# An earlier gather for the first expert, and the first attention heads in another order

## The chip, the cores and the metric

The kernel runs on one core of a Trainium2 chip. Its time is the device time of one execution in microseconds (us). TensorE (PE, with its weight loads as PEld), VectorE (DVE), ScalarE (ACT) and GpSimd (POOL) each work through their own instructions in order; SyncE (SP) issues most of the DMAs, also in order.

## The reference

Three stages, each feeding the next, all in float32.

```
scores = q @ k.T / 8 + (cum[i] - cum[j]),  cum = cumsum(log(clip(f, 1e-4, 1)))   # 4 batches, 8 heads, 576 rows, 64 wide
attn   = softmax over j <= i;  x = attn @ v          -> (2304, 512)
x      = (sigmoid(x @ w_gate) * (x @ w_val)) @ w_out -> (2304, 512), 1536 wide inside
logits = x @ moe2_w_gate                             -> (2304, 8)
# all 18432 (token, expert) pairs in falling order of logit: a pair is taken
# if the token is still free and the expert has under 288 tokens
out[tokens of e] = relu(x[tokens of e] @ w1[e]) @ w2[e]      # 8 experts, 512 -> 1024 -> 512
```

## The kernel before

Products that need more than one pass of precision are made from a high part (`hi`, rounded to fp32r) and a rest (`lo`), as hi·hi + hi·lo + lo·hi.

**Attention** (`attention`) goes through 32 heads. For a head, `load` brings q and k of a pair of heads into `raw` (576 KB), `prep` (ACT, L128) rounds them into `P1`, `prep2` (POOL, L141 and L142) forms the rest in `P2`, and `copies` (SP, L136 and L137) sends `P1` to the other half of `P2`. `P1` has three more rows: two of the decay (`cum`, split in two) or of ones, and a third that holds the negated row maxima. `maxpass` multiplies q by k in blocks into three PSUM banks and takes row maxima on DVE (L169); `mrows` turns them on PE, ACT copies them (L176), and `mstore` (SP, L179) writes them into row 66 of `P1`. Only then can `scores` run for that head: PE multiplies, ACT takes exp (L199), POOL zeroes what lies above the diagonal (L203). `av` multiplies by v. In the steady part one pass of the loop issues scores of head h, then av of head h-1 with the maxima of head h+3 placed between its matmuls. The first heads are written out by hand ahead of the loop; the order of the whole attention is the order of the code, on each engine. `warm` issues matmuls into a bank that nobody reads. `fill` places the first steps of the next stage's weights between heads: `W.load` (SP, L386, 512 KB each), `W.bits` (three DVE steps, L394 to L400), `W.cut` (ACT L408, POOL L411).

**Feed-forward** (`Ffn`) keeps the weights in SBUF, and works in five groups of tokens. The last product of the last 6 token tiles is put off: `defer` is a generator of 252 matmul steps (L666), each tile 36 steps, the last tile (tokens 15 of 18) as two halves of 36. Its result is copied by ACT (L669) into `xd` and stored to `x2d` in DRAM (L513).

**Routing** (`Route`) finds the assignment by 7 rounds on DVE and PE; `filler` puts deferred matmuls between them. `permutation` writes `idx`, the token numbers of each expert. Beside the rounds, `EW.split` prepares the first four weight tiles of the first expert.

**Experts** (`experts`): three indirect DMAs on POOL (`gather`, L991) fetch the 288 tokens of an expert from `x2d` in pieces of 96, PE turns them (`turn`, L1001), ACT and DVE split them (L1004, L1005), then two layers follow (L1015, L1028). A `gather` waits for every earlier store into `x2d`. For the first expert it stands behind the last store; 27 matmuls (L1056) that nobody reads stand on PE meanwhile. Four more weight tiles are loaded by ACT's queue (L949) behind the turned tokens, and split by ACT, POOL and DVE (L971, L973) during the first layer.

Of the kernel before, what the change touches and what calls it, by code (L numbers as in the profile page):

```python
# [34 lines left out]
def make_consts(ev, pool, keep):  # L35

    nc = ev.nc

    jp = pool.tile([128, 128], I32, name="jp")
    nc.gpsimd.iota(jp, pattern=[[1, 128]], base=0, channel_multiplier=-1)  # L40
    ev.identb = pool.tile([128, 128], BF16, name="identb")
    nc.vector.tensor_scalar(ev.identb, jp, 0.0, None, op0=OP.is_equal)
    ev.mk = pool.tile([128, 512], BF16, name="mk")
    nc.vector.memset(ev.mk, 1.0)
# [16 lines left out]
WARM = (22, 4, 2, 2)  # L61
# [3 lines left out]
def attention(ev, qkT, vr, f, xs, rec, ckd, fill):  # L65
# [4 lines left out]
    with ExitStack() as ctx:  # L70
# [27 lines left out]
        zero = st.tile([NHEAD, 1], F32, name="zero")  # L98
        nc.gpsimd.memset(zero, 0.0)
        next(consts)  # L100
# [8 lines left out]
        ck = st.tile([NHEAD, 2, S], F32R, name="ck")  # L109
        nc.vector.tensor_scalar(ft, ft, 1e-4, 1.0, op0=OP.max, op1=OP.min)  # L110
        nc.scalar.activation(ft, ft, AF.Ln)
        next(consts)
# [4 lines left out]
        for t in P1[2:]:  # L117
            nc.vector.memset(t[64:67].bitcast(F32), 1.0)
# [32 lines left out]
        def maxpass(h):  # L151

            p1 = P1[h % 4]
            a = ps1.tile([128, 512], F32, name="p1b")
            c = ps1.tile([128, 512], F32, name="p1b")
            b = MT[h] = ps2.tile([128, 1024], F32, name="pb")
            q = lambda s, e: p1[0:66, Q0 + s:Q0 + e]
            k = lambda s, e: p1[0:66, K0 + s:K0 + e]
# [3 lines left out]
            mm(c[:, 448:512], q(-64, 64), k(0, 64), False, True)  # L162
            mm(b[:, 256:512], q(448, 576), k(0, 256), True, True)
            mm(b[:, 512:832], q(448, 576), k(256, 576), True, True)
            mx = MR[h] = wk.tile([128, 5], F32R, name="mx", bufs=3)
            for t, src in ((1, a[:, 0:192]), (2, a[:, 192:512]), (3, c[:, 0:448]), (0, c[:, 448:512]),
                           (4, b[:, 256:832])):
                n = src.shape[-1]
                nc.vector.tensor_tensor_reduce(out=junk[:, JT[t]:JT[t] + n], in0=src, in1=ev.mq[:, S - n:], op0=OP.add,  # L169
                                               op1=OP.min, scale=-1.0, scalar=3e38, accum_out=mx[:, t:t + 1])  # L170
# [76 lines left out]
        def warm(n):  # L247

            t = ps2.tile([128, 1024], F32, name="pv")
            for _ in range(n):  # L250
                mm(t[:, 0:512], ev.identb, ev.mk, True, True)
# [7 lines left out]
        idle = st.tile([NHEAD, 1], F32, name="warm")  # L259
# [12 lines left out]
        prep2(1)  # L272
        ones(2)
        ones(0)
        for h in (2, 3):
            prep(h)
# [15 lines left out]
        load_v(1)  # L292
        load(3)
        decays(3)
        for h in range(1, NHEAD):
            odd = h % 2
            scores(h, 3 if h == 2 else None)
            if h == 2:
                mstore(3)
                next(consts)  # L300

            def rows(r):
                if r < NHEAD:
                    mrows(r)
                    mstore(r)

            def early():
                rows(h + 2 if h > 1 else 2)
                if h + 4 < NHEAD:
                    prep(h + 4)  # L310

            def late():
                if h + 3 < NHEAD:
                    maxpass(h + 3)

            if h == 1:
                av(0, {2: early, 3: lambda: maxpass(3)})
            elif h == 2:
                av(1, {0: lambda: maxpass(4), 5: early})
                late()  # L320
            else:
                av(h - 1, {AT[0]: early, AT[1]: late})
            if h < NHEAD - 3:
                copies(h + 3)
            if h >= 3 and odd:
                store(h // 2 - 1)
            if not odd and h // 2 + 3 < NPAIR:
                load(h // 2 + 3)
                decays(h // 2 + 3)
            if odd and h // 2 + 2 < NPAIR:  # L330
                load_v(h // 2 + 2)
# [6 lines left out]
            if h in (1, 2):  # L338
                fill(h - 3)
            fill(h)  # L340
# [361 lines left out]
class Route:  # L702
# [195 lines left out]
    def permutation(self, a):  # L898
# [5 lines left out]
        st = wk.tile([128, 2, NT], F32, name="r_st", bufs=1)  # L904
        nc.vector.tensor_reduce(st[:, 0], sl.rearrange("p e t -> p t e"), op=OP.add, axis=AX.X)
# [18 lines left out]
        return idx  # L924


class Experts:
# [9 lines left out]
    def load(self, n, queue=None):  # L937
        queue = queue or self.ev.nc.sync
        e, i = divmod(n, 8)
        if e < E:  # L940
            if n < 4:
                r = self.raw[n] = self.first.tile([128, 1024], F32, name="fraw", bufs=2)
            else:
                r = self.raw[n] = self.pool.tile([128, 1024], F32, name="eraw", bufs=RAWS)
            if i < 4:
                queue.dma_start(r, self.w1[e, i * 128:(i + 1) * 128, :])
            else:
                i -= 4
                queue.dma_start(r.rearrange("p (k d) -> p k d", k=2),  # L949
                                          self.w2[e, i * 256:(i + 1) * 256, :].rearrange("(k p) d -> p k d", p=128))  # L950

    def split(self, n, part=None, after=None):

        if part is not None:
# [7 lines left out]
            if part:  # L962
                del self.raw[n]
                if n < 2:
                    self.load(n + 2)
# [12 lines left out]
WAIT = 27  # L978


def experts(ev, W, x2d, idx, out, wk, psum):
    nc = ev.nc
    XG, XE, Y, T = {}, {}, {}, {}
# [11 lines left out]
    def turn(e, k, p=None, tiles=(0, 1, 2)):  # L995
        if k == 0 and tiles[0] == 0:
            XE[e] = [wk.tile([128, 4, CH], F32R, name=n) for n in ("xeh", "xel")]
        xh, xl = XE[e]
        p = p or psum("t")
        for i in tiles:  # L1000
            nc.tensor.transpose(p[:, i * TT:(i + 1) * TT], XG[e][i][:, k * 128:(k + 1) * 128], ev.ident[:TT, :TT])  # L1001
        if tiles[-1] < 2:
            return
# [53 lines left out]
    p = [psum(n) for n in "ttty"]  # L1057
    for i in range(3):
        for k in range(4):
            turn(0, k, p[k], (i,))  # L1060
# [39 lines left out]
def network(tc, qk, vv, f, ww, bcT, w1, w2, cb, cf, out):  # L1100
# [3 lines left out]
    with ExitStack() as ctx:  # L1104
# [25 lines left out]
        def fill(h):  # L1130
# [8 lines left out]
            count = lambda h: 3 + (h - 3) * (EARLY - 1) * 3 // 27  # L1139
            jobs = lambda h: range(count(h), count(h + 1))  # L1140
            for lag, do in enumerate((W.bits, lambda n, s: s == 2 and W.cut(n, (0,)),
                                      lambda n, s: s == 2 and W.cut(n, (1,)))):
                if 3 <= h - lag < 30:
# [33 lines left out]
        rest = F.defer(xd)  # L1177

        def filler(n):
            for _ in range(n):  # L1180
                if next(rest, 0) == 0:
                    break

        R = Route(ev, rp, rw, F.bank, cb, cf, scratch, filler)
        EW.load(0)
        EW.load(1)
# [15 lines left out]
        experts(ev, EW, x2d, ev.idx, out, xw, lambda n: pools[n].tile([128, 512], F32, name="e" + n))  # L1202
# [30 lines left out]
```

## Time and profile before

| | us |
|---|---|
| three runs | 935.55, 935.75, 939.06; median 935.75 |
| profiled execution, its own time | 935.39 |
| span of that execution | 933.4 |
| PE busy in the span | 911.9 (98%) |

A row of a group or of the timeline is one line of the kernel on one engine, what it writes and reads, how often, and how long it was busy. A bracket at its end says how long the engine stood idle before it and what released it. SPq, ACTq and POOLq rows are the issuing of DMAs. The granted clock of PE is given as a share of 2.4 GHz: 1.00 is 2.4 GHz, 0.50 is 1.2 GHz.

### The profile page before, as it was taken

How to read it: one execution, taken by the hardware profiler on the slowest of the kernel's cores; microseconds unless marked ns; L12 is line 12 of the kernel's file. 1: busy time of each engine (PE TensorE's matmuls, PEld its weight loads, DVE VectorE, ACT ScalarE, POOL GpSimd, SP SyncE). 2: the span in 40 equal slices, each digit the busy share in tenths (PEclk: the TensorE clock that was granted, in tenths of full speed). 3: DMA queues.
4: the chain of work that ended last, by engine and by line, in shares of the span. 5: the costliest groups of instructions: out<-in, count | busy, mean ns of one | idle time of the engine just before them, and what ended most of it. 6: DMA issues, size and time to landing. Idle time of an engine off the chain costs nothing. (4 is left out here: it accounts for less than half of the span.)

```text
span 933.4 us, 14077 instructions
## 1 busy us (share of the span) xinstructions
PE 911.9 (98%) x5187; PEld 767.1 (82%) x5188; DVE 550.2 (59%) x1188; ACT 330.7 (35%) x570; POOL 456.3 (49%) x388
## 2 busy tenths in 40 slices
PE   7999999999999999999999999999989999999996
PEld 4677777778788888888888888887779999999995
DVE  6467879736887287997979642535504433434431
ACT  4366666652323112121121221221116544444530
POOL 5578888853566113221222221322138787777641
PEclk7699999999999999999999999999999999999998
DMA  5688898764553202101021210011128765656610
GB/s 124 143 217 218 210 226 230 201 170 149 161 162 107 74 0 71 38 19 56 17 76 41 65 46 1 1 55 46 47 82 268 223 188 176 201 179 199 204 41 26
DMA packets 48873, 111.04 MB, mean 119 GB/s; under 512 B 11331, under 2 KB 11747, under 8 KB 48803
## 3 DMA queue, kind: packets, MB, share of 16 engines
q1 hardware_dynamic: 44642, 98.59, 37.7%
q0 software_dynamic: 3072, 9.44, 3.0%
q10 hardware_dynamic: 1088, 2.10, 0.7%
q8 instruction: 41, 0.67, 0.3%
q14 instruction: 30, 0.24, 0.1%
HBM read 86.12 MB, written 14.45 MB: 108 GB/s over the span
## 5 line engine op out<-in xcount | busy, mean ns | idle before, releaser
L497 POOL TENSOR_TENSOR gl<-sg,gh 128x512 fp32r<-128x512 f32 x36 | 50.0, 1388 | 200.9 <-ACT gh L496 200.9
L973 POOL TENSOR_TENSOR elo<-eraw,ehi 128x1024 fp32r<-128x1024 f32 x45 | 108.1, 2411 | 42.3 <-ACT ehi L971 41.9
L145 PE MATMUL pv<-e,vf 128*65 128x256 f32 (+1 forms) x434 | 108.6, 376 | 0.0
L490 PE MATMUL gv<-xah,w_hi 128*128 128x512 f32 (+1 forms) x288 | 103.3, 359 | 0.0
L490 PE MATMUL gv<-xal,w_hi 128*128 128x512 f32 (+1 forms) x288 | 103.0, 358 | 0.0
L490 PE MATMUL gv<-xah,w_lo 128*128 128x512 f32 (+1 forms) x288 | 102.9, 357 | 0.0
L530 DVE CUSTOM_DVE_ANT_0 mb<-mb,bc 128x512 f32<-128x512 f32 x96 | 82.2, 856 | 3.3
L530 DVE CUSTOM_DVE_ANT_0 mb<-mr,bc 128x512 f32<-128x512 f32 x96 | 82.4, 858 | 2.8
L1015 PE MATMUL eh<-xeh,ehi 128*128 128x288 f32 x256 | 78.8, 308 | 0.1
L496 ACT ACTIVATE gh<-sg 128x512 fp32r<-128x512 f32 x36 | 22.8, 633 | 156.5 <-PE o L509 84.4
L1028 PE MATMUL ey<-hh,ehi 128*128 128x288 f32 x256 | 78.1, 305 | 0.0
L1015 PE MATMUL eh<-xel,ehi 128*128 128x288 f32 x256 | 77.0, 301 | 0.0
L1015 PE MATMUL eh<-xeh,elo 128*128 128x288 f32 x256 | 76.8, 300 | 0.0
L1028 PE MATMUL ey<-hl,ehi 128*128 128x288 f32 x256 | 76.5, 299 | 0.0
L490 PE MATMUL gv<-xbh,w_hi 128*128 128x512 f32 x192 | 76.2, 397 | 0.0
L490 PE MATMUL gv<-xbl,w_hi 128*128 128x512 f32 x192 | 76.1, 396 | 0.0
L490 PE MATMUL gv<-xbh,w_lo 128*128 128x512 f32 x192 | 76.1, 396 | 0.0
L1028 PE MATMUL ey<-hh,elo 128*128 128x288 f32 x256 | 75.8, 296 | 0.0
L169 DVE CUSTOM_DVE_ANT_0 mj<-p1b,mq 128x192 bf16<-128x192 f32 (+3 forms) x128 | 46.8, 420 | 47.1 <-PE p1b L145 47.1
L145 PE MATMUL p1b<-P 66*128 66x192 f32 (+7 forms) x256 | 69.4, 340 | 2.8 <-DMA P<-ck 1.5
L145 PEld LDWEIGHTS pv<-e,vf 128*65 128x65 f32 x434 | 51.4, 142 | 24.9 <-issue 16.7
L1018 DVE SCALAR_TENSOR_TENSOR hl<-eh,hh 128x288 fp32r<-128x288 f32 x64 | 29.1, 456 | 61.6 <-ACT hh L1017 61.6
(204 smaller groups left out, 2285.2 us busy)
## 6 DMA issues: line engine op xcount, KB each, us to landing
eraw<-w SPq DMA_DIRECT2D x56, 512.0 KB
mr<-ww SPq DMA_DIRECT2D x26, 512.0 KB
raw<-qk SPq DMA_DIRECT2D x16, 576.0 KB
p<-P SPq DMA_DIRECT2D x64, 144.0 KB
vf<-vv SPq DMA_DIRECT2D x16, 330.0 KB
bc<-ww SPq DMA_DIRECT2D x10, 512.0 KB
xs<-xo SPq DMA_DIRECT2D x16, 292.5 KB
xr<-rec SPq DMA_DIRECT2D x32, 128.0 KB
```

Source lines behind the costliest of these rows:

```text
L145: nc.tensor.matmul(out, lhsT, rhs, start=start, stop=stop, skip_group_check=True)
L169: nc.vector.tensor_tensor_reduce(out=junk[:, JT[t]:JT[t] + n], in0=src, in1=ev.mq[:, S - n:], op0=OP.add, op1=OP.min, scale=-1.0, scalar=3 ...
L490: nc.tensor.matmul(p[i][:, :m], w_[:, ws], x_[:, k], start=n == 0, stop=n == 11)
L496: nc.scalar.activation(hi, s, AF.Copy)
L497: nc.gpsimd.tensor_tensor(lo, s, hi, op=OP.subtract)
L530: nc.vector.tensor_tensor_reduce(out=junk, in0=a, in1=self.bc[j], op0=OP.mult, op1=OP.add, scale=1.0, scalar=0.0, accum_out=res)
L973: eng.tensor_tensor(lo, r, hi, op=OP.subtract)
L1015: nc.tensor.matmul(p[:, :CH], w_[:, ws], x_[:, k], start=n == 0, stop=n == 11)
L1018: nc.vector.scalar_tensor_tensor(h[1][:, f], p[:, :CH], 0.0, h[0][:, f], op0=OP.max, op1=OP.subtract)
L1028: nc.tensor.matmul(p[:, :CH], w_[:, ws], h_[:, f], start=n == 0, stop=n == 23)
```

## The change

Two places change; lines of the changed code have other numbers, since it is 43 lines longer.

At the head of attention: the ones in `P1` are set by POOL and no longer by DVE; the constant tile `mk` goes (the warm matmuls read the identity instead); ACT runs one small Ln ahead of the first real one; 19, 4, 6, 2 warm matmuls stand where 22, 4, 2, 2 stood; the maxima of head 1 are issued in two parts with `mrows` of head 0 between them; `prep` and `copies` of heads 2 to 4, the memsets `ones` and the loads of pair 3 and of v change places; the first weight loads and their steps move from ahead of heads 1, 1 and 2 to the ends of heads 2, 4 and 5, and the later weight steps begin at head 5 and not 3 (42 steps over 25 heads, not 27).

At the first expert: zeros are stored into the rows of token tile 15 in `x2d` early, the gather of the first expert is issued when the two halves of tile 15 are still to be multiplied, and its missing rows are added by a matmul of `xd` with a 0/1 matrix `hot`. This turn uses ordinary float32 matmuls with the identity, not transposes. The 27 matmuls go. `fraw`, which holds raw weights of the first expert, has one buffer and not two.

```
-WARM = (22, 4, 2, 2)
+FIRST = {2: -3, 4: -2, 5: -1}
+WARM = (19, 4, 6, 2)
...
         for t in P1:
+            nc.gpsimd.memset(t[64:67].bitcast(F32), 1.0)
             nc.gpsimd.memset(t[0:64, 0:64].bitcast(F32), 0.0)
-        for t in P1[:2]:
-            nc.vector.memset(t[64:67].bitcast(F32), 1.0)
...
+        ones(1)
         copies(0)
+        prep2(0)
         maxpass(0)
         warm(WARM[1])
-        prep2(0)
-        ones(1)
         decays(1)
         copies(1)
+        prep2(1)
+        first = maxparts(1)
+        next(first)
         mrows(0)
         mstore(0)
-        maxpass(1)
+        next(first)
+        prep(2)
+        prep2(2)
         warm(WARM[2])
-        prep2(1)
-        ones(2)
-        ones(0)
-        for h in (2, 3):
-            prep(h)
         mrows(1)
         mstore(1)
         scores(0)
-        maxpass(2)
-        warm(WARM[3])
+        prep(3)
         load_v(0)
-        load(2)
         copies(2)
         decays(2)
-        for h in (2, 3):
-            prep2(h)
+        load(2)
         copies(3)
-        prep(4)
-        prep2(4)
-        fill(-3)
-        load_v(1)
-        load(3)
-        decays(3)
+        warm(WARM[3])
+        maxpass(2)
+        prep2(3)
+        ones(2)
...
+            if h in FIRST:
+                fill(FIRST[h])
...
+        self.xg = [t[:TT] for t in (slots[:, :DM], slots[:, DM:], big)]
...
+    def gather(self, route):
+        for i in range(3):
+            nc.gpsimd.indirect_dma_start(out=self.xg[i], out_offset=None, in_=self.x2d, ...)
+        nc.gpsimd.iota(places, pattern=[[1, CH]], base=0, channel_multiplier=0)
+        nc.vector.tensor_scalar(self.hot[:, :CH], places, route.slot[:, LAST:LAST + 1], None, op0=OP.is_equal)
+    def turn(self, x, bank):
+        for k in range(4):
+            ks = slice(k * 128, (k + 1) * 128)
+            p = bank()
+            for i in range(3):
+                nc.tensor.matmul(p[:, i * TT:(i + 1) * TT], self.xg[i][:, ks], self.ev.ident[:TT, :TT], start=i == 0, ...)
+            nc.tensor.matmul(p[:, :CH], x[:, ks], self.hot[:, :CH], start=False, stop=True, skip_group_check=True)
+            nc.scalar.activation(self.x[0][:, k], p[:, :CH], AF.Copy)
+            nc.vector.tensor_tensor(self.x[1][:, k], p[:, :CH], self.x[0][:, k], op=OP.subtract)
...
-    gather(0)
-    p = psum("h")
-    for _ in range(WAIT):
-        nc.tensor.matmul(p, W.hi[0][:, :128], W.hi[0][:, :512], start=True, stop=True)
...
+        nc.vector.memset(xd, 0.0)
+        F.store(LAST, xd)
...
+        filler(left - 2 * 3 * NF)
+        X0 = First(ev, ep, scratch, x2d)
+        X0.gather(R)
         for part in range(2):
             EW.split(3, part, ev.idx[:1, :1])
-        filler(1000)
+        filler(left)
+        next(rest, 0)
+        X0.turn(xd, F.bank)
```

What stood on PE at the maxima of heads 0 and 1, before (`P_0`, `P_1` are the operands of heads 0 and 1, `mx` the maxima, `pv<-mk,identb` a warm matmul):

```order
L145 MATMUL pv<-mk,identb 128x512
L145 MATMUL pb<-identr,mx 5x128
L145 MATMUL p1b<-P_1_117 128x192
L145 MATMUL p1b<-P_1_117 128x320
L145 MATMUL p1b<-P_1_117 128x448
L145 MATMUL p1b<-P_1_117 128x64
L145 MATMUL pb<-P_1_117 128x256
L145 MATMUL pb<-P_1_117 128x320
```

And in the changed kernel:

```order
L143 MATMUL pv<-identb 128x512
L143 MATMUL p1b<-P_1_117 128x192
L143 MATMUL p1b<-P_1_117 128x320
L143 MATMUL p1b<-P_1_117 128x448
L143 MATMUL p1b<-P_1_117 128x64
L143 MATMUL pb<-identr,mx 5x128
L143 MATMUL pb<-P_1_117 128x256
L143 MATMUL pb<-P_1_117 128x320
```

The turning of head 0's maxima moved behind four of head 1's matmuls.

What SP issued before head 2's maxima (`P_2_118<-mr`), before; `mr<-ww` is a weight load, `raw` a load of q and k, `vf` one of v, `p_...<-P` a copy:

```order
L136 DMA p_230<-P_3_119 64x576
L137 DMA p_230<-P_3_119 64x576
L386 DMA mr_290<-ww 128x512
L386 DMA mr_292<-ww 128x512
L93 DMA vf<-vv 128x660
L84 DMA raw_103<-qk 64x2x1152
L89 DMA raw_103<-ckd 2x2x576
L179 DMA P_2_118<-mr 1x5x128
```

And in the changed kernel:

```order
L83 DMA raw_105<-qk 64x2x1152
L134 DMA p_255<-P_3_119 64x576
L135 DMA p_255<-P_3_119 64x576
L188 DMA P_2_118<-mr 1x5x128
L134 DMA p_315<-P_0_116 64x576
L135 DMA p_315<-P_0_116 64x576
L83 DMA raw_103<-qk 64x2x1152
L88 DMA raw_103<-ckd 2x2x576
L92 DMA vf<-vv 128x660
```

Two weight loads, one of v and one of q and k moved from ahead of head 2's maxima to behind them.

What stands on PE in the changed kernel between the last turned k-block and the first expert's first layer (`mr` are the gathered tokens and `xd`, `mb` is `hot`):

```order
L1020 MATMUL gv<-ident,mr_5456 128x96 x2
L1020 MATMUL gv<-ident,mr_5455 128x96
L1022 MATMUL gv<-mb_5458,mr_5455 128x288
L1059 MATMUL eh<-xe0h,ehi_5597 128x288
L1059 MATMUL eh<-xe0l,ehi_5597 128x288
L1059 MATMUL eh<-xe0h,elo_5598 128x288
```

Each of four such k-blocks has three matmuls with the identity and one with `hot`, and the deferred matmuls stand right ahead of the first.

## Rows read from the trace of the kernel before

**Rows 1.** The page's first part: busy us, share of the span, instructions.

```profile
PE 911.9 (98%) x5187; PEld 767.1 (82%) x5188; DVE 550.2 (59%) x1188; ACT 330.7 (35%) x570; POOL 456.3 (49%) x388
```

**Rows 2.** Waits of PE over the span: us in total, times, longest us.

```profile
PE et L1001 <- DMA xg<-x2d,idx: 3.0, 3, 1.7
...
PE p1b L145 <- DVE mx L169: 1.1, 1, 1.1
```

**Rows 3.** Stretches of 1 us: PE, PEld, DVE, ACT, POOL busy; then clock, DMA, GB/s.

```profile
13.00:14.00 1.00, 0.65 (x3) 0.65 (x4) 0.29 (x2) 0.34 (x2) 0.94 (x2) 0.50 0.40 97
...
33.00:34.00 1.00, 0.40 (x1) 0.00 (x0) 1.00 (x1) 0.56 (x1) 0.93 (x2) 0.77 1.01 203
...
37.00:38.00 1.00, 1.00 (x6) 0.97 (x6) 0.00 (x0) 0.70 (x2) 0.00 (x0) 0.50 0.16 51
...
43.00:44.00 1.00, 1.00 (x5) 0.48 (x3) 0.00 (x0) 0.00 (x0) 0.00 (x0) 0.65 0.00 0
```

**Rows 4.** Timeline of PE, first heads: start us, us busy, line, operation.

```profile
10.50 0.74 PE L145 MATMUL p1b<-P 66*128 66x192 f32 x4 [1.54 <-DMA P<-ck]
...
13.35 0.27 PE L145 MATMUL pb<-identr,mx 128*5 128x128 f32 x1 [0.89 <-DVE mx L169]
...
16.57 0.52 PE L145 MATMUL py<-P 67*128 67x256 f32 x1
...
35.68 0.39 PE L145 MATMUL py<-P 67*128 67x256 f32 x1 [2.28 <-DMA P<-mr]
...
45.74 0.28 PE L145 MATMUL py<-P 67*128 67x256 f32 x1
...
47.50 1.13 PE L145 MATMUL pv<-e,vf 128*65 128x256 f32 x4
...
56.73 0.52 PE L145 MATMUL py<-P 67*128 67x256 f32 x1
```

**Rows 5.** Timelines of DVE, ACT and SP in the same stretch.

```profile
4.66 0.45 DVE L110 TENSOR_SCALAR ft<-ft 32x576 f32<-32x576 f32 x1
...
7.72 0.75 DVE L116 SCALAR_TENSOR_TENSOR ck<-cum,ck 32x576 fp32r<-32x576 f32 x1
...
6.96 2.22 ACT L128 ACTIVATE P<-raw 64x1152 fp32r<-64x1152 f32 x2 [1.13 <-DMA raw<-qk]
...
0.82 0.40 SPq L77 DMA_DIRECT2D ft<-f  x1
...
8.49 1.46 SPq L132 DMA_DIRECT2D P<-ck  x2
...
28.71 0.76 SPq L179 DMA_DIRECT2D P<-mr  x1
```

**Rows 6.** Timeline of PE at the first expert.

```profile
622.76 1.50 PE L653 MATMUL gv<-fold,mr 16*128 16x8 f32 x12
...
685.40 6.32 PE L1056 MATMUL eh<-ehi 128*128 128x512 f32 x27
...
695.86 0.74 PE L1001 MATMUL et<-ident,xg 96*128 96x96 f32 x3 [0.68 <-DMA xg<-x2d,idx]
...
696.78 0.61 PE L1015 MATMUL eh<-xeh,ehi 128*128 128x288 f32 x1
```

**Rows 7.** Timelines of ACT and POOL there.

```profile
677.02 0.60 ACT L669 ACTIVATE mr<-o 128x512 f32<-128x512 f32 x1 [6.42 <-PE o L666]
...
685.60 0.38 ACT L669 ACTIVATE mr<-o 128x256 f32<-128x256 f32 x1 [3.88 <-PE o L666]
...
690.04 1.13 POOL L991 DMA_INDIRECT xg<-x2d,idx  x1 [10.53 <-issue]
...
692.70 0.92 POOL L991 DMA_INDIRECT xg<-x2d,idx  x1 [0.31 <-issue]
```

**Rows 8.** Stretches of 2 us at the first expert, columns as in rows 3.

```profile
694.00:696.00 2.00, 0.69 (x5) 0.51 (x6) 0.00 (x0) 0.00 (x0) 1.46 (x2) 0.91 0.44 121
...
702.00:704.00 2.00, 2.00 (x15) 2.00 (x15) 0.46 (x1) 1.18 (x3) 1.60 (x1) 0.88 1.01 271
```

More of the change, by code (lines that the diff above doesn't have):

```diff
@@ L98, in attention @@
         zero = st.tile([NHEAD, 1], F32, name="zero")
+        idle = st.tile([NHEAD, 1], F32, name="warm")
         nc.gpsimd.memset(zero, 0.0)
+        nc.scalar.activation(idle, zero, AF.Ln, bias=1.0)
         next(consts)
@@ L162, in maxpass @@
             mm(c[:, 448:512], q(-64, 64), k(0, 64), False, True)
+            for t, src in ((1, a[:, 0:192]), (2, a[:, 192:512]), (3, c[:, 0:448]), (0, c[:, 448:512])):
+                top(t, src)
+            yield
+            b = MT[h] = ps2.tile([128, 1024], F32, name="pb")
             mm(b[:, 256:512], q(448, 576), k(0, 256), True, True)
             mm(b[:, 512:832], q(448, 576), k(256, 576), True, True)
[L165 to L170, printed above, removed]
+            top(4, b[:, 256:832])
+            yield
+        def maxpass(h):
+            for _ in maxparts(h):
+                pass
         def mrows(h):
@@ L297, in attention @@
             scores(h, 3 if h == 2 else None)
+            if h == 1:
+                ones(0)
             if h == 2:
@@ L308, in early @@
                 rows(h + 2 if h > 1 else 2)
-                if h + 4 < NHEAD:
+                if h == 1:
+                    prep(4)
+                    prep2(4)
+                elif h + 4 < NHEAD:
                     prep(h + 4)
@@ L317, in attention @@
                 av(0, {2: early, 3: lambda: maxpass(3)})
+                prep(5)
             elif h == 2:
@@ L326, in attention @@
                 store(h // 2 - 1)
+            if h == 1:
+                load(3)
+                decays(3)
             if not odd and h // 2 + 3 < NPAIR:
@@ L941, in load @@
             if n < 4:
-                r = self.raw[n] = self.first.tile([128, 1024], F32, name="fraw", bufs=2)
+                r = self.raw[n] = self.first.tile([128, 1024], F32, name="fraw", bufs=1)
             else:
@@ L963, in split @@
                 del self.raw[n]
-                if n < 2:
-                    self.load(n + 2)
+                if n < 3:
+                    self.load(n + 1)
         elif n < 8 * E:
@@ L977, with __init__, experts @@
 RAWS = 4
-WAIT = 27
-def experts(ev, W, x2d, idx, out, wk, psum):
+LAST = 15
+class First:
+    def __init__(self, ev, pool, scratch, x2d):
+        nc = self.nc = ev.nc
+        big, slots, self.places, self.hot = scratch
+        self.ev, self.x2d = ev, x2d
+        self.xg = [t[:TT] for t in (slots[:, :DM], slots[:, DM:], big)]
+        self.x = [pool.tile([128, 4, CH], F32R, name=n) for n in ("xe0h", "xe0l")]
+    def gather(self, route):
+        nc = self.nc
+        for i in range(3):
+            nc.gpsimd.indirect_dma_start(out=self.xg[i], out_offset=None, in_=self.x2d,
+                                         in_offset=bass.IndirectOffsetOnAxis(ap=self.ev.idx[:, i:i + 1], axis=0))
+        places = self.places[:, :CH].bitcast(I32)
+        nc.gpsimd.iota(places, pattern=[[1, CH]], base=0, channel_multiplier=0)
+        nc.vector.tensor_scalar(self.hot[:, :CH], places, route.slot[:, LAST:LAST + 1], None, op0=OP.is_equal)
+    def turn(self, x, bank):
+        nc = self.nc
+        for k in range(4):
+            ks = slice(k * 128, (k + 1) * 128)
+            p = bank()
+            for i in range(3):
+                nc.tensor.matmul(p[:, i * TT:(i + 1) * TT], self.xg[i][:, ks], self.ev.ident[:TT, :TT], start=i == 0,
+                                 stop=False, skip_group_check=True)
+            nc.tensor.matmul(p[:, :CH], x[:, ks], self.hot[:, :CH], start=False, stop=True, skip_group_check=True)
+            nc.scalar.activation(self.x[0][:, k], p[:, :CH], AF.Copy)
+            nc.vector.tensor_tensor(self.x[1][:, k], p[:, :CH], self.x[0][:, k], op=OP.subtract)
+def experts(ev, W, x2d, first, idx, out, wk, psum):
     nc = ev.nc
-    XG, XE, Y, T = {}, {}, {}, {}
+    XG, XE, Y, T = {}, {0: first}, {}, {}
     scattered = []
@@ L993, in gather, with turn @@
             XG[e].append(x)
-    def turn(e, k, p=None, tiles=(0, 1, 2)):
-        if k == 0 and tiles[0] == 0:
+    def turn(e, k):
+        if k == 0:
             XE[e] = [wk.tile([128, 4, CH], F32R, name=n) for n in ("xeh", "xel")]
         xh, xl = XE[e]
-        p = p or psum("t")
-        for i in tiles:
+        p = psum("t")
+        for i in range(3):
             nc.tensor.transpose(p[:, i * TT:(i + 1) * TT], XG[e][i][:, k * 128:(k + 1) * 128], ev.ident[:TT, :TT])
-        if tiles[-1] < 2:
-            return
         nc.scalar.activation(xh[:, k], p[:, :CH], AF.Copy)
@@ L1176, in network @@
         EW = Experts(ev, ep, w1, w2)
-        rest = F.defer(xd)
+        rest, left = F.defer(xd), 7 * 3 * NF
         def filler(n):
-            for _ in range(n):
-                if next(rest, 0) == 0:
-                    break
+            nonlocal left
+            for _ in range(min(n, left)):
+                next(rest, 0)
+                left -= 1
+        nc.vector.memset(xd, 0.0)
+        F.store(LAST, xd)
         R = Route(ev, rp, rw, F.bank, cb, cf, scratch, filler)
         EW.load(0)
-        EW.load(1)
         F.logits(scratch[1], filler)
```

40 lines of the change are left out of this document (17 added, 23 removed).

## The prediction

> **What bounds the kernel now.** I read the page's first part, then PE's waits, then stretches and timelines of the two places that the change touches. PE is busy for 98% of the span, no other engine for over 59% [rows 1]. The longest entry among PE's waits is 3.0 us [rows 2], so there is little idle time to win. What is left is time in which PE ran slowly or did work that nobody reads. The clock rows show the first: PE was granted 0.50 from 13 us on, was back at full speed within the stretch from 33, at 0.50 again in the stretch from 37 and back within that from 43 [rows 3]. Three gaps stand ahead of these falls: 1.54 and 0.89 us before the first, 2.28 us before the second [rows 4]. From 45.74 to 56.73 two heads take 11.0 us, 5.5 each, with 1.76 us of it for the scores [rows 4]; but from the scores of head 0 (16.57) to those of head 3 (45.74) 29.2 us go by, where three heads at full speed would take 16.5. That is a loss of some 12 us. The second place is the first expert: the deferred matmuls end at 685.40, the first layer starts at 696.78 [rows 6], with 6.32 us of idle matmuls, the gather and its waits between, and the clock falls at its end and is back within the stretch from 702 [rows 8].
>
> **The start, part by part.** *Decay.* The clamp of `ft` starts at 4.66 on DVE, right behind two memsets of `P1` and that of `mk`, all of which leave DVE. What is then late is the arrival of `ft`, issued at 0.82. The trace does not show when it lands. The nearest row is the small DMA `P<-ck`: issued at 8.49, in use on PE at 10.50, 2.0 us [rows 4, 5]. `ft` is larger, so I take 3.3 (ends: 2.4, when DVE is free, and 4.66, as now). From the clamp to the end of `ck` 3.81 us pass (7.72 + 0.75 - 4.66), so `ck` is ready at 7.1, not 8.47. The decay's DMA then lies behind the load of pair 1 in SP's queue, and lands, I estimate, at 9.4. `prep` of head 0 is done by 8.1 (half of 2.22 from 6.96), so the first maxima start at 9.4 and not 10.50. POOL now sets four tiles of ones, about 1.1 us each by what DVE took for as many elements per row, all done by 8.1 when its first `prep2` can start: free, and about 1 us late if POOL needs more.
>
> *Maxima.* From the first maxima to `mrows` of head 0, 2.85 us go by (10.50 to 13.35) [rows 4]. That puts it at 12.25; four matmuls of head 1 and four warm ones stand ahead of it and cover all but about 0.5 us of the wait for DVE. ACT's copy, the second part of head 1, its maxima on DVE and six warm matmuls that cover them follow: scores of head 0 start at about 15.0, not 16.57.
>
> *Heads 0 to 3 at full speed.* Scores 0 to 2, maxima 2 to 5 and av 0 and 1 are two heads (11.0), one more scores (1.76) and two more maxima (the first four blocks, 1024 of 1600 columns, take 0.74 [rows 4], so 1.16 each): 15.1 us. I add waits of 2.3: two warm matmuls 0.5; head 2's maxima row 0.5; 0.3 for the exponentials of head 0; and 1.0 before the maxima of head 4, since ACT now does `prep` of heads 4 and 5 (1.1 each) and the copy of av 0 ahead of the exponentials of head 2. `prep` of head 4 also waits for `ones(2)` on POOL, behind four `prep2`. Scores of head 3 then start at 32.4 instead of 45.74: 13.3 us earlier. This is the upper end.
>
> *The wait of 2.28 us.* `P<-mr` of head 2 was issued at 28.71 and needed until 35.68 [rows 4, 5], since two weight loads, one of v and one of q and k (1.9 MB) had been issued just before it in the same queue. In the changed order it follows 576 KB of q and k and one head's copies. At about 215 GB/s, near the 203 of the row from 33 [rows 3], everything issued from vf of pair 0 to there (1.5 MB) takes 7 us from about 16.8, so it lands at 24 to 24.5, and scores 2 wait 0.5 us at full speed, none at half. The bulk loads are late next: they stand ahead of the rows of heads 3 and 5, which are needed 6 and 10 us after, about as long as these loads take.
>
> *The lower end.* If the clock falls at 13 as now and stays down until the av of head 0 ends, nothing is won to 33.4 [rows 3], except that scores 2 then start at once: scores 1.8, ACT's wait 1.2, two maxima 2.3 and av 2.6 (5.5 less 1.76 and 1.16) bring head 3 at 41.3: 4.4 us earlier.
>
> *The value.* The gaps before head 0's scores shrink from 2.4 to about 1.9 us (1.4 and 0.5), and PE does full-speed warm work on both sides of them; I take it that the clock holds there. But a second group of waits (0.5 and 1.0 us at 24 to 27) lies where it may fall, and a fall like that of 37 to 43 costs 6.7 us at half speed, 3.3 us [rows 3]. So 13.3 - 3.3 = **10.0 us** for the start.
>
> **The first expert.** Now the last ACT copy (685.60 + 0.38) frees the last store, and the first gather starts 4.06 us later, at 690.04; the third starts 2.66 us after the first, and its data let PE go on at 695.86, 3.16 us after its issue [rows 6, 7]. In the changed kernel the store that the gather waits for is that of the tile before, copied by 677.62. The same steps give a first gather at 681.7, the third at 684.3, landed at 687.5. PE's deferred matmuls end at 685.4 as before, so PE waits about 2 us with six small matmuls in it.
>
> The Trainium skill ("DMA: Bandwidth & Descriptors", Anatomy of one DMA) puts a DMA at about 2.0 us plus its bytes over 436 GB/s; for this store of 256 KB that is an estimate of 2.6 us where the row has 4.06, and by it the gather would land at 686.0 and the sum would be 1.5 us better. The measured 4.06 decides.
>
> Then the turn. A float32 matmul with these shapes isn't in the trace. The nearest rows are six float32 matmuls in 12 records, 1.50 us, so 0.25 a matmul of few columns [rows 6]; a block of four is 1.0 us (ends: 0.6 at the transposes' rate, 1.5 if the 288 columns of `hot` come on top at half speed). After 687.5: the rest of the first block 0.7, three more 3.0, and ACT and DVE on the last block 1.15, since the first matmul of the layer takes a bank of the turn and waits for DVE: layer 1 starts at 692.35, not 696.78: **4.4 us** (3 to 6). POOL issues the gathers before it splits the last weight tile, which ends at 688.6, in time; one `fraw` buffer makes tile 1's load wait until 643, and ACT has nothing else to do until 656. The weights of layer 2 are issued behind the turned tokens, as before. With the gap, I take the clock to fall as before, at equal cost.
>
> Sum: 14.4 us off the profiled execution's 935.39, which lies 0.36 under the median: 935.75 - 14.4 = 921.35. I forecast **921.5**.
>
> **Rivals.**
> *The clock falls at 13 all the same* and stays down until av 0: 4.4 at the start and 4.4 at the expert, 8.8: 926.9. For it: 1.4 us of the gap stays, since raw data come no sooner than 6.96 [rows 5]; against it: the second gap halves.
> *No fall at either place:* 13.3 + 4.4 + 3.4 (half of the 6.8 us from 695.6 to 702.5, where the clock shares of the two stretches put the fall and the rise [rows 8]) = 21.1: 914.7. For it: PE has work in most of the time; against it: 2 us without tokens at 685.
> *The early gather isn't early:* if it still ends behind the last store or POOL is late with it, only the start counts, 10.0: 925.7. For it: POOL, one engine, carries the gathers, `hot`'s numbers and the split. Against it: it is issued ahead of 72 matmuls that take 8.5 us.
> *Slower:* the weight steps are squeezed from 27 heads into 25, so more of them stand ahead of maxima on DVE. One such wait of 1.1 us shows in the span [rows 2]. If every one of the 25 heads paid it, 27.5 us less 14.4 would be lost: 948.9. It decides from 13 heads on. Against it: the rate grows by 8% only, and DVE is at 59% [rows 1].
>
> **How the numbers follow.** Forecast 0.36, clock falls at 13 0.27, no fall 0.17, gather not early 0.09, slower by DVE 0.04, several small waits that leave 0 to 5 us of gain (933) 0.07. 0.5% is 4.7 us, about what a measurement of this kernel can tell from no change. Faster: all of the first four, less a share where two losses meet: 0.88; same 0.08; slower 0.04. The range leaves out part of the no-fall case below and the last two above: 914 to 931; the forecast's own is 918 to 925 (the ends of `ft`, of the turn and of the waits).
>
> **What would show it.** Right: scores of head 3 near 36 us; no wait of 2 us on `P<-mr`; `ck` done near 7; one stretch of half speed before 45 us and not two; the first gather some 4 us after the copy of the tile before the last; layer 1 some 7 us after the last deferred matmul, and not 11.4. Wrong: 0.50 from 13 to 33 again; a wait on the token tiles at 690; more than a few waits on DVE's maxima between 50 and 200 us.

## The result, and the profile after

The changed kernel takes 922.61 us (median of 4 runs, 920.94 to 924.52), the kernel before 935.65 (4 runs, 935.34 to 939.06): 13.0 us less by the medians. The ratio of the two kernels is 0.9845, 95% interval 0.9819 to 0.9871 (the two medians alone give 0.9861). The forecast was 921.5 in a range of 914 to 931. The execution profiled is the slowest of the four, 924.52 us, 10.9 less than the profiled one of before.

PE's share hasn't changed [rows 1]; PE is busy 10.4 us less. First part of the page of the changed kernel:

```profile
PE 901.5 (98%) x5182; PEld 758.9 (82%) x5182; DVE 548.7 (59%) x1185; ACT 330.7 (36%) x571; POOL 459.9 (50%) x393
```

PE's waits over the span, changed kernel: the 3.0 us on the token tiles [rows 2] are 0.6; new or longer are, above all, the waits on the rest of the turned tokens (`xe0l`, at layer 1), on ACT's exponentials, on v and on `hot` (`mb`, L1011).

```profile
PE py L143 <- DMA P<-mr: 1.7, 1, 1.7
PE eh L1059 <- DVE xe0l L1024: 1.0, 1, 1.0
PE p1b L143 <- ACT e L208: 0.9, 1, 0.9
PE pv L143 <- DMA vf<-vv: 0.8, 1, 0.8
PE p1b L143 <- DVE mx L159: 0.8, 1, 0.8
PE gv L1022 <- DVE mb L1011: 0.8, 1, 0.8
PE gv L1020 <- DMA mr<-x2d,idx: 0.6, 1, 0.6
```

The start, timeline of PE (L143 was L145), answering to [rows 4]:

```profile
9.84 0.73 PE L143 MATMUL p1b<-P 66*128 66x192 f32 x4 [1.79 <-DMA P<-ck]
...
25.74 0.39 PE L143 MATMUL py<-P 67*128 67x256 f32 x1 [1.67 <-DMA P<-mr]
...
28.66 1.28 PE L143 MATMUL p1b<-P 66*128 66x192 f32 x4 [0.92 <-ACT e L208]
...
36.87 0.28 PE L143 MATMUL py<-P 67*128 67x256 f32 x1
```

The rows at 25.74 and 36.87 are the scores of heads 2 and 3: 9.9 and 8.9 us earlier than before. The clock, in stretches of 1 us as in [rows 3], is up at 13, falls at 29 and is back in the stretch from 35:

```profile
13.00:14.00 1.00, 0.85 (x5) 0.54 (x6) 1.00 (x7) 1.00 (x2) 0.90 (x1) 1.00 0.96 221
...
29.00:30.00 1.00, 1.00 (x5) 0.81 (x4) 0.74 (x5) 0.23 (x2) 0.97 (x1) 0.51 0.30 74
...
35.00:36.00 1.00, 1.00 (x5) 0.57 (x3) 0.00 (x0) 1.00 (x2) 0.00 (x0) 0.58 0.00 0
```

The first expert, timelines of PE, DVE and POOL (the turn is now L1020 and L1022, layer 1 L1059), answering to [rows 6, 7]:

```profile
676.85 0.28 PE L678 MATMUL o<-w_lo,w_hi 128*128 128x256 f32 x1
...
678.12 0.46 PE L1020 MATMUL gv<-ident,mr 96*128 96x96 f32 x2 [0.57 <-DMA mr<-x2d,idx]
679.36 0.72 PE L1022 MATMUL gv<-mb,mr 128*128 128x288 f32 x2 [0.78 <-DVE mb L1011]
...
682.41 1.22 PE L1022 MATMUL gv<-mb,mr 128*128 128x288 f32 x2
...
684.65 1.22 PE L1022 MATMUL gv<-mb,mr 128*128 128x288 f32 x2
686.87 0.61 PE L1059 MATMUL eh<-xe0h,ehi 128*128 128x288 f32 x1 [0.99 <-DVE xe0l L1024]
...
676.38 2.83 DVE L1011 TENSOR_SCALAR mb<-mb,r_st 128x288 f32<-128x288 int32 x1 [8.23 <-POOL mb L1010]
...
672.36 1.13 POOL L1007 DMA_INDIRECT mr<-x2d,idx  x1 [15.62 <-issue]
...
676.44 1.26 POOL L973 TENSOR_TENSOR elo<-fraw,ehi 128x512 fp32r<-128x512 f32 x1
...
677.79 1.25 POOL L973 TENSOR_TENSOR elo<-fraw,ehi 128x512 fp32r<-128x512 f32 x1
```

The gather is early, and the tokens are there at 678.12. But the turn waits for `hot`, and its blocks take 2.24 us (682.41 to 684.65), since the clock falls in it; stretches of 2 us:

```profile
680.00:682.00 2.00, 2.00 (x14) 1.80 (x12) 0.59 (x2) 0.82 (x2) 0.94 (x1) 0.74 0.04 8
...
690.00:692.00 2.00, 2.00 (x13) 2.00 (x13) 0.46 (x1) 1.36 (x2) 0.41 (x1) 0.70 1.06 406
```

From the last deferred matmul to layer 1 (the handover) it is 10.0 us, 11.5 before. Of the 10.9 us between the two profiles 8.9 are there at the scores of head 3, 8.4 at the last deferred matmul, and 9.9 at layer 1. The long stretch between the first two places varies by itself: it takes 638.1 to 641.9 us over the fourteen profiles of this document.

### The profile page after: what moved, and what is told of

It is laid out like the page before. It is cut to its first block, busy times and chain, and to the rows that moved or that the text cites. A ratio compares the mean times of both kernels' runs of the same rounds, so it can differ in the third digit from the quotient of the medians.

```text
span 922.6 us, 14053 instructions
## 1 busy us (share of the span) xinstructions
PE 901.5 (98%) x5182; PEld 758.9 (82%) x5182; DVE 548.7 (59%) x1185; ACT 330.7 (36%) x571; POOL 459.9 (50%) x393
## 5 line engine op out<-in xcount | busy, mean ns | idle before, releaser
L143 PE MATMUL pv<-e,vf 128*65 128x256 f32 (+1 forms) x434 | 106.5, 370 | 0.8 <-DMA vf<-vv 0.8
L143 PEld LDWEIGHTS pv<-e,vf 128*65 128x65 f32 x434 | 50.3, 139 | 25.1 <-issue 15.4
L143 PE MATMUL p1b<-P 66*128 66x192 f32 (+7 forms) x256 | 66.0, 326 | 3.5 <-DMA P<-ck 1.8
L1059 PE MATMUL eh<-xeh,ehi 128*128 128x288 f32 x224 | 67.8, 303 | 0.0
L1059 PE MATMUL eh<-xeh,elo 128*128 128x288 f32 x224 | 66.3, 296 | 0.0
L1059 PE MATMUL eh<-xel,ehi 128*128 128x288 f32 x224 | 66.3, 296 | 0.0
```

Source lines behind the costliest of these rows:

```text
L143: nc.tensor.matmul(out, lhsT, rhs, start=start, stop=stop, skip_group_check=True)
L1059: nc.tensor.matmul(p[:, :CH], w_[:, ws], x_[:, k], start=n == 0, stop=n == 11)
```

## The experiments

The table has for each kernel the median, the ratio to the kernel before on the same chip with its 95% interval, and three places of its profile: start of the scores of heads 2 and 3, and the way from the start of the last deferred matmul to layer 1 (us).

| kernel | median | ratio | head 2 | head 3 | to layer 1 |
|---|---|---|---|---|---|
| before | 935.65 | | 35.68 | 45.74 | 11.50 |
| changed | 922.61 | 0.9845 (0.9819 to 0.9871) | 25.74 | 36.87 | 10.02 |
| start_only | 924.65 | 0.9866 (0.9838 to 0.9894) | 25.50 | 35.99 | 11.37 |
| expert_only | 931.46 | 0.9931 (0.9903 to 0.9958) | 35.57 | 46.79 | 9.37 |
| hot_early | 923.42 | 0.9850 (0.9824 to 0.9877) | 26.12 | 36.18 | 6.66 |
| warm_rows | 921.24 | 0.9836 (0.9809 to 0.9864) | 27.21 | 34.52 | 7.71 |
| copy4_only | 936.80 | 1.0003 (0.9986 to 1.002) | 35.93 | 46.60 | 11.29 |
| copy4_back | 927.24 | 0.9901 (0.9872 to 0.9929) | 31.55 | 42.95 | 11.00 |
| bulk_back | 928.88 | 0.9919 (0.9893 to 0.9945) | 34.53 | 44.84 | 9.35 |
| both | 918.91 | 0.9821 (0.9792 to 0.9850) | 27.09 | 34.39 | 6.62 |
| after_again | 920.69 | 0.9826 (0.9798 to 0.9855) | 25.44 | 35.68 | 7.71 |
| copies_later | 918.04 | 0.9793 (0.9761 to 0.9825) | 25.64 | 33.80 | 6.55 |
| small_back | 920.96 | 0.9820 (0.9792 to 0.9847) | 28.15 | 36.20 | 9.36 |
| no_warm | 924.70 | 0.9865 (0.9833 to 0.9896) | 27.96 | 37.87 | 10.99 |

The first four after "changed" ran on one chip (before: 937.37), the next four on one (937.03), the last four on one (938.15). Medians are compared within such a group, ratios across groups.

### The two parts apart

`start_only` has the changed lines up to the end of attention and in the weight steps' count, `expert_only` the others.

> The changed attention with the first expert of before. Theory (the two parts are independent and the start carries most): scores of head 3 near 36.9 us as in the changed kernel, layer 1 some 11.4 us after the last deferred matmul as before, time 8.9 us under before, 926 to 927.5. Rival (as forecast, the handover is worth 4.4 us): what is left here is 13.0 - 4.4 = 8.6 us, 927, and the other run tells. Rival (the parts disturb each other): less than 7 us, above 928.5.

> The attention of before with the changed first expert. Theory (the handover turns its tokens at half clock, as the profile of the changed kernel shows): layer 1 some 9.9 us after the last deferred matmul, 0.50 from the turn on for about 10 us, time 2.0 to 2.8 us under before: 933. Rival (as forecast): layer 1 some 7 us after the last deferred matmul, 4.4 us under before: 931.2.

The start alone is worth 12.7 us, more than the 8.9 expected (its scores of head 3 are 9.8 us earlier than before), the expert alone 5.9 (intervals 9.9 to 15.2 and 3.9 to 9.1); both together 13.0 in the first comparison and 17.5 in the last. So they don't disturb each other beyond what can be measured. For `expert_only` the one theory had 2.0 to 2.8 us of gain, the other 4.4: the interval lies above the first and holds the second, though layer 1 comes 9.37 us after the last deferred matmul in the profile, not 7. By chance the run shows more: it has the attention of before, instruction for instruction, and in this execution the clock did not fall at 13, but at 27. Stretches of 1 us of `expert_only`, two ahead of its first fall:

```profile
13.00:14.00 1.00, 0.65 (x5) 0.64 (x6) 0.31 (x3) 0.39 (x2) 0.94 (x2) 1.00 0.40 97
...
22.00:23.00 1.00, 1.00 (x7) 0.43 (x4) 0.00 (x0) 0.00 (x0) 0.93 (x2) 1.00 1.02 230
```

Its timelines of PE and then of ACT, from the end of that stretch on:

```profile
28.87 1.28 PE L145 MATMUL p1b<-P 66*128 66x192 f32 x4 [5.83 <-ACT e L199]
...
35.57 0.58 PE L145 MATMUL py<-P 67*128 67x256 f32 x1 [1.41 <-DMA P<-mr]
...
46.79 0.28 PE L145 MATMUL py<-P 67*128 67x256 f32 x1
...
26.63 1.17 ACT L128 ACTIVATE P<-raw 66x1152 fp32r<-66x1152 f32 x1 [7.86 <-DMA raw<-ckd]
27.70 0.63 ACT L199 ACTIVATE e<-py 128x576 f32<-128x576 f32 x1
```

At full speed PE was through by 23 and then stood for 5.83 us; the scores of head 2 came at 35.57, against 35.68 in the profile with half speed from 13 to 33 [rows 3, 4]. Up to there the first fall cost nothing. (From 28 to 44 the clock was at 0.50 here, and the scores of head 3 came at 46.79, against 45.74.) What held PE was ACT: its copy of head 4 waited until 26.63 for raw rows, with the exponentials of head 1 behind it.

### Which edits carry the start

`copy4_only` is the kernel before with this alone, and `copy4_back` the changed kernel with it undone:

```
-        prep(4)              # ahead of the loop over heads
-        prep2(4)
...
+                if h == 1:   # within av(0), behind the exponentials of head 1
+                    prep(4)
+                    prep2(4)
...
+                prep(5)      # behind av(0)
```

> The kernel before with one edit: ACT's copy of head 4 (and its DMA) behind the exponentials of head 1, in the first steps of head 0's sums, and that of head 5 behind them. Theory A (in the kernel before, ACT's copy of head 4 waits for its raw rows until 25 to 27 us and holds the exponentials of head 1 behind it; the half speed from 13 on cost nothing, since PE would have idled instead): exponentials of head 1 near 20 instead of 27, scores of head 2 at 30 to 33 instead of 35.7, where the row of maxima behind the bulk loads is next, scores of head 3 at 40 to 43, 3 to 5 us less than before. Theory B (as forecast, the time is lost by the clock): scores of head 3 stay near 45.7, less than 1 us.

> The changed kernel with the copies of head 4 and head 5 back at their places of before. Theory A: ACT waits for the raw rows until near 25 with the exponentials of head 1 behind it, as in before; sums of head 0 end near 28 instead of 24, scores of head 3 at 40 to 42 instead of 36.9, 3 to 5 us more than the changed kernel: 926 to 928. Theory B (only the order of the loads and the clock count): less than 1 us more, 923.5.

`bulk_back` is the changed kernel with `fill(-3)`, `load_v(1)`, `load(3)` and `decays(3)` back behind `copies(3)`.

> The changed kernel with the first two weight tiles, one tile of v and the q, k of pair 3 (1.3 MB) back ahead of the row of maxima of head 2 in SP's queue. Theory (the loads ahead of it set when that row lands): the row lands 4 to 6 us later, the wait ahead of the scores of head 2 is 5 to 7 us instead of 1.7, scores of head 3 at 40 to 42, 3 to 5 us more: 926 to 928. Rival (the row doesn't wait for the loads): within 1 us, 923.

Timeline of PE of `copy4_only`, the scores of head 2:

```profile
35.93 0.58 PE L145 MATMUL py<-P 67*128 67x256 f32 x1 [5.43 <-DMA P<-mr]
```

Timeline of PE of `copy4_back`, the maxima of head 3 in the middle of head 0's sums:

```profile
26.93 1.28 PE L143 MATMUL p1b<-P 66*128 66x192 f32 x4 [5.51 <-ACT e L208]
```

Timelines of PE and SP of `bulk_back`, the scores of head 2, the issue of the first weight tiles, and that of the row of maxima behind them:

```profile
34.53 0.58 PE L143 MATMUL py<-P 67*128 67x256 f32 x1 [10.47 <-DMA P<-mr]
...
20.31 1.16 SPq L399 DMA_DIRECT2D mr<-ww  x2
...
24.50 0.76 SPq L188 DMA_DIRECT2D P<-mr  x1
```

By its two numbers `copy4_only` fits theory B: the scores of head 3 stay at 46.60, and 936.80 is no gain (theory A had 3 to 5 us). Its trace shows A's mechanism: the exponentials of head 1 did come before ACT's copy, but at 23.9 and not 20, and the time saved turned wholly into the next wait, 5.43 us on the row of maxima, which was issued at 28.01 behind the bulk loads and used at 35.93. The granted clock was 1.00 from 28 until after 33, so PE's clock is not what held the scores of head 2.

`copy4_back` and `bulk_back` refute the rivals. By their ratios they lose 5 to 7 us and 7 to 9 us against the changed kernel (0.9845, and 0.9826 in `after_again`; no run of it stands in their group). `bulk_back` came out worse than expected (wait of 10.47 us for 5 to 7, scores of head 3 at 44.84 for 40 to 42): the loads put back are 1.9 MB (twice 512 KB, 330 and 576 KB), not the 1.3 MB of the expectation. The DMA engines were busy throughout from 21 to 33 us there (share 0.95 to 1.15 in each stretch of 1 us), so the run doesn't tell whether the row waits in SP's queue or for the DMA engines; no run issues it from another queue.

So two limits stood one on the other: ACT's copy until 27, the row behind the loads until 35.7. Lifting ACT's alone gives nothing; the queue's alone was not run. With the rest of the change in place, the scores of head 3 are 2.8 us earlier than before without ACT's edit (`copy4_back`), 0.9 without the queue's (`bulk_back`), and 8.9 to 10.1 with both.

`small_back` undoes the two small edits: ones by DVE, maxima of head 1 in one piece.

```
         for t in P1:
-            nc.gpsimd.memset(t[64:67].bitcast(F32), 1.0)
             nc.gpsimd.memset(t[0:64, 0:64].bitcast(F32), 0.0)
+        for t in P1[:2]:
+            nc.vector.memset(t[64:67].bitcast(F32), 1.0)
...
+        for t in P1[2:]:
+            nc.vector.memset(t[64:67].bitcast(F32), 1.0)
...
-        first = maxparts(1)
-        next(first)
         mrows(0)
         mstore(0)
-        next(first)
+        maxpass(1)
```

> The changed kernel with the two smaller edits undone: the ones of all four tiles by DVE (two of them ahead of the clamp) and the maxima of head 1 in one piece behind the row of head 0. Theory (the start up to 24 us is not what ends last: the row of maxima and the raw rows of pair 2 are, through SP's queue): scores of head 0 1 to 1.5 us later, as before the change, scores of head 3 0.5 to 1.5 us later, time 0.5 to 1.5 us more: 923 to 924. Rival (the two edits carry the start): 4 us or more, 926.6 or more.

`no_warm` has `WARM = (1, 0, 0, 0)`.

> The changed kernel with one idle matmul instead of 31. Theory (the first 24 us wait for data and not for PE): clock 0.50 up to 20 us or longer, scores of head 2 still at 25 to 27 behind the row of maxima, the price is what half speed costs behind that: 1 to 4 us more, 923.5 to 926.5. Rival (as forecast, a low clock from 13 on costs 5.6 us): 928.

`small_back` takes 920.96 against 920.69 for the changed kernel in the same group: no difference that can be measured, and the rival is refuted. Its stretches of 2 us and timeline of PE:

```profile
14.00:16.00 2.00, 2.00 (x8) 1.33 (x7) 1.63 (x9) 1.03 (x1) 1.05 (x2) 0.50 0.49 112
...
17.89 0.52 PE L146 MATMUL py<-P 67*128 67x256 f32 x1
...
28.15 0.39 PE L146 MATMUL py<-P 67*128 67x256 f32 x1 [0.21 <-DMA P<-mr]
...
36.20 0.39 PE L146 MATMUL py<-P 67*128 67x256 f32 x1
```

Its scores of head 0 start at 17.89, 2.9 us late, with the clock at 0.50 from 13 to 20. The theory would have this delay vanish in the wait for the row of maxima. That wait did shrink to 0.21 us, but the scores of head 2 are still 2.7 us later than in `after_again`. Head 3 starts within 0.7 us of both profiles of the changed kernel because the clock, having fallen at 13, did not fall again near 27 to 29: from the scores of head 2 to those of head 3 it takes 8.05 us, against 10.24 in `after_again` and 11.13 in the first profile. So the level time does not show that the start up to 24 us is free.

Without idle matmuls the kernel is 4.0 us slower, the upper end of what was expected. Its scores of head 2 are 2.5 us and those of head 3 2.2 us later than in `after_again`; its profiled execution also has the long handover.

### The handover, and the clock

`hot_early` puts the iota and the comparison ahead of the three gathers; `warm_rows` puts idle matmuls into PE's two waits; `both` has the two edits.

```
+            if h == 2:
+                warm(4)
             scores(h, 3 if h == 2 else None)
...
             elif h == 2:
+                warm(3)
                 av(1, {0: lambda: maxpass(4), 5: early})
```

> The changed kernel; the numbers of places and the comparison that makes the one-hot tile stand ahead of the three gathers instead of behind them. Theory (the comparison, 2.83 us beside POOL's split, comes 0.78 us late, and the gap of PE around it lets the clock fall): the comparison takes under 1 us near 670, no wait for it at the turn, clock 1.00 through the turn, blocks of 1.2 us instead of 2.24, layer 1 near 683.5 instead of 686.9, and full speed behind it, 4 to 5.5 us less: 917 to 918.5. Rival (the small matmuls of the turn and the wait for the gathers let the clock fall without it): only the 0.8 us of the wait go, 0.50 from near 681 as now: 921.8.

> The changed kernel with four idle matmuls of 512 columns ahead of the scores of head 2 and three ahead of the maxima of head 4 (0.24 us each at full speed, in the waits of 1.67 and 0.92 us). Theory (those two waits make the clock fall at 29): clock 1.00 through to 40, scores of head 3 near 33.5 instead of 36.9, 3 to 3.5 us less: 919.3. Rival (the clock falls near 29 with or without them): time as the changed kernel, 922 to 923.5, scores of head 3 at 36.9 or later.

> The changed kernel with the seven idle matmuls in the waits of head 2's scores and head 4's maxima, and the comparison of the one-hot tile ahead of the gathers. Theory (fewer and shorter gaps keep the clock up in more executions): mean granted clock 0.995 to 0.998 in most executions, handover of 6.7 us, time 918 to 920. Rival (where the clock falls is chance of the execution and the edits don't bear on it): mean clocks spread from 0.987 to 0.998 as in the kernels without them, 921.5 to 923.

> The changed kernel, unchanged, a second time. If where the clock falls belongs to the program, the profile shows 0.50 from 29 to 36 and from 681 to 691 again and a handover of 10 us. If it belongs to the execution, one of the two is missing or lies elsewhere; a handover at full speed takes 7.7 us (the wait for the one-hot tile stays). Time 921 to 924, mean clocks 0.987 to 0.993.

In `hot_early` the comparison takes 0.36 us, PE doesn't wait for it, and a block of the turn takes 1.16 us. Its timelines of DVE and PE:

```profile
668.54 0.36 DVE L1008 TENSOR_SCALAR mb<-mb,r_st 128x288 f32<-128x288 int32 x1
...
678.84 0.68 PE L1022 MATMUL gv<-mb,mr 128*128 128x288 f32 x2
...
679.99 0.68 PE L1022 MATMUL gv<-mb,mr 128*128 128x288 f32 x2
...
683.98 0.40 PE L1059 MATMUL eh<-xe0h,ehi 128*128 128x288 f32 x1 [0.99 <-DVE xe0l L1024]
```

But `after_again`, the changed kernel a second time, has the late comparison and the same two waits, and there the clock held. Its timeline of PE:

```profile
675.25 0.46 PE L1020 MATMUL gv<-ident,mr 96*128 96x96 f32 x2 [0.57 <-DMA mr<-x2d,idx]
676.50 0.72 PE L1022 MATMUL gv<-mb,mr 128*128 128x288 f32 x2 [0.79 <-DVE mb L1011]
...
681.69 0.40 PE L1059 MATMUL eh<-xe0h,ehi 128*128 128x288 f32 x1 [0.99 <-DVE xe0l L1024]
```

So the same waits of the same program let it fall in one execution and not in another. (Whether the two ran on one chip is not known; on one chip too executions differ, with mean clocks of 0.992 to 0.998 in `warm_rows`.) Over the eleven profiles with the changed expert: with the comparison late it fell in 6 of 8 (9.35 to 11.0 us to layer 1) and held in 2 (7.71); with it early it held in 3 of 3 (6.55 to 6.66). The wait itself is 0.8 us; that it also brings the falls is likely, not shown by 3 profiles. In time the gain of 4 to 5.5 us did not come: 923.42 for `hot_early` is within 1 us of the changed kernel. Its profiled execution is the fastest of its five, at a mean clock of 0.994; the four others have 0.990 to 0.992, so the clock was down for longer in them, at places that no profile shows.

With idle matmuls at the waits of 24 to 29 the clock stays at 1.00 up to 46 us in all three profiles that have them (`warm_rows`, `both`, `copies_later`); in the four with the same start and without them (changed, `after_again`, `start_only`, `hot_early`) it fell between 26.9 and 29.0. The scores of head 3 came at 34.5 in `warm_rows`, short of the 33.5 expected, since the matmuls themselves had to wait for a PSUM tile that ACT copied late. The time followed less: 921.24 for 919.3 expected, 0.8 us under the changed kernel by the ratios, which can't be told from none. `both` comes out as its theory had it, with 918.91 and mean clocks of 0.994 to 0.996 in five of six executions; by the ratios that is 1.4 us under `warm_rows` and 2.7 us under `hot_early`, within their intervals. A stretch of 1 us and the timeline of PE of `warm_rows`:

```profile
29.00:30.00 1.00, 1.00 (x9) 0.68 (x8) 0.00 (x0) 1.00 (x3) 1.00 (x1) 1.00 0.43 97
...
26.54 1.02 PE L143 MATMUL pv<-identb 128*128 128x512 bf16 x4 [2.46 <-ACT xo L238]
```

`copies_later` mends this: it is `hot_early` with the four idle matmuls, and

```
                 av(0, {2: early, 3: lambda: maxpass(3)})
+                prep(4)      # was within av(0), ahead of ACT's copy of its sums
+                prep2(4)
...
             scores(h, 3 if h == 2 else None)
+            if h == 2:
+                prep(5)      # was ahead of the exponentials of head 2
+                prep2(5)
```

> The kernel with the one-hot tile early and four idle matmuls ahead of the scores of head 2; ACT's copy of head 4 now behind that of head 0's sums, and that of head 5 behind the exponentials of head 2. Theory (ACT's two copies of 1.16 us ahead of the exponentials are what PE waits for at 24 to 29): the idle matmuls start near 24.8 and not at 26.5, scores of head 2 near 25.8, no wait ahead of the maxima of head 4, scores of head 3 at 32.5 to 33 instead of 34.4, 1.5 us under the kernel with the seven idle matmuls: 917 to 918. Rival (head 5's rows come late now): a wait of 1 to 2 us ahead of the maxima of head 5 or the scores of head 4 takes it back, 919.

Its timeline of PE, idle matmuls and the scores of head 3:

```profile
24.81 1.02 PE L143 MATMUL pv<-identb 128*128 128x512 bf16 x4 [0.73 <-ACT xo L238]
...
33.80 0.39 PE L143 MATMUL py<-P 67*128 67x256 f32 x1 [0.81 <-DMA P<-mr]
```

The idle matmuls, the scores of head 2 (25.64) and the maxima of head 4, without a wait, are where they were expected, and a part came back as a wait of 0.81 us on head 3's row. Its median, 918.04, is 2.7 us under the changed kernel's 920.69 in the same group, and its ratio to before, 0.9793, is the best of all. The runs overlap (915.26 to 921.07 against 919.03 to 924.35).

## Why the prediction was right, and where it was not

The time (922.61 for 921.5) and the likeliest case were right: one fall ahead of 45 us, a gather that is early. Its two terms were 10.0 and 4.4; by the profiles of the changed kernel the start gave 8.9 and 10.1, the handover 1.5 and 3.8. That the median came within 1.1 us of the forecast is in part luck: the two terms add up to 10.4 us in one profile and 13.9 in the other, and which it is hangs on whether the clock falls in the handover; the sum took that fall at the cost it had before.

*What bounds the start.* Here the reasoning failed though the number held. I read the 12 us as lost by a slow clock. `expert_only` shows that the first half-speed stretch, 13 to 33, cost nothing up to the scores of head 2 (35.57 without it, 35.68 with it), and `copy4_back` and `bulk_back` what did: the order on ACT and of SP's loads. The number held all the same, since the sum for the new order (15.0, 15.1 and 2.3) was added up along that order and doesn't use this reading. I had both orders before me, and priced the queue's ("The wait of 2.28 us") at what PE waited, where 5.4 to 10.5 us stood behind it once PE was early.

*Up to the scores of head 0.* `ck` was ready at 7.74 (forecast 7.1), the first maxima at 9.84 (9.4), the row of head 0 at 12.57 (12.25), its scores at 15.01 (15.0). The data landed before the 3.3 that I took: the clamp starts at 2.70. But it lasts 1.34 us and not 0.45 [rows 5], beside POOL's memsets, which I had called free. Whether this stretch counts in the time stays open: `small_back`, 2.9 us later here, is level, but with one fall of the clock in place of another; `no_warm`, with PE at half-speed pace up to 23 us, is 4.0 us slower.

*The rows of head 2* arrived at 25.74, not 24 to 24.5, and cost a wait of 1.67 us and not 0.5; the 1.0 us ahead of the maxima of head 4 is 0.92. *The clock* held at the first gaps though the first of them grew to 1.79 us, and fell at 29, for 6.8 us where 6.7 were forecast. "Scores of head 3 near 36": 36.87 and 35.68.

*The rival "the clock falls at 13 all the same"* was given 5.6 us. No run shows that price: in the changed order no profile has the clock down from 13 until the av of head 0 ends. In `small_back` it fell at 13, was back by 20, and the time is level. The reading behind the price was wrong, as above. *The rival of the weight steps on DVE* is refuted: from 45 to 300 us PE waits 0.8 us on maxima, and not at all in `after_again`, as against 1.1 before.

*The expert.* The first gather came 3.17 us after ACT's copy of the tile before the last had ended (669.19 to 672.36), where I took 4.06 from [rows 7]. So the tokens came a microsecond after the last deferred matmul and not two. The formula of the Trainium skill ("DMA: Bandwidth & Descriptors", Anatomy of one DMA) is given there for DMAs that GpSimd issues, while SP issues this store; the estimate of 2.6 by it was too low, as 4.06 was too high. Mis-sized was the turn: `hot`, which I did not price, came 0.78 us late; a block takes 1.16 us at full speed (forecast 1.0) and 2.24 at half speed, and the clock fell inside the turn and not, as I assumed, at equal cost behind it. Layer 1 came 10.0 us after the last deferred matmul (forecast 7); with the clock up 7.7, and with `hot` early 6.6.

## What to carry to other kernels

When an engine at half speed is ready no later than what it waits for next, its slow clock costs nothing: look for the wait that would take its place before putting a price on the clock. In-order queues stack their limits, so a single reordering can measure as nothing and still be needed for a gain of 9 us; test such edits by undoing them from the good version as well. A small operation put beside a busy neighbour, here a comparison of 0.36 us that took 2.83, must be priced where it stands. A time that stays level when an edit is undone doesn't prove that stretch free: look in the trace for what made up for it.

## What the runs showed of the hardware

- A DVE operation can be held for as long as POOL works: the comparison took 2.83 us beside POOL's two subtractions (it ended 0.17 us after the second), and 2.83 in all eight profiles where it stands there; alone it took 0.36 us (`hot_early`, `both`). The Trainium skill ("SBUF — State Buffer", SBUF: two separate sides) speaks of one pair of ports that POOL and some operations of DVE lock against each other for a whole instruction; the rows agree that DVE waits, but here the hold lasted over two instructions of POOL. The clamp shows a hold with POOL's memsets (one runs from 2.63 to 3.73): 1.34 us for 0.45 [rows 5]. Not every operation is held: the scan of `cum` took 1.34 us beside memsets and 1.35 in the kernel before, without them. Timeline of DVE of the changed kernel, the clamp:

```profile
2.70 1.34 DVE L111 TENSOR_SCALAR ft<-ft 32x576 f32<-32x576 f32 x1
```

- The granted clock is not all that sets PE's pace: in `no_warm` the column shows 1.00 from 10 to 23 us, and the matmuls there take as long as others at 0.50. A stretch of 1 us of `no_warm`:

```profile
20.00:21.00 1.00, 1.00 (x6) 0.99 (x5) 0.83 (x7) 0.47 (x1) 0.85 (x3) 1.00 0.81 122
```

  A matmul of 320 columns from its timeline of PE; in `expert_only` at full speed such a one takes 0.31 us, in the kernel before at 0.50 0.47 us:

```profile
15.97 0.47 PE L143 MATMUL py<-P 67*128 67x320 f32 x1
```

- Whether the clock falls at a gap differs between executions of one program: the two profiles of the changed kernel have the same waits there (0.57 us, and 0.78 or 0.79), and 10.0 and 7.7 us of handover.
